# Loading the first block of Wk in two halves, and running its matmuls ahead of the second tile's transposes

## The chip, the core and the metric

The kernel runs on one core of a Trainium2 chip. The metric is the time of one execution on the device in microseconds (us); the median of seven executions stands for the kernel. A core has five engines that run side by side, each with its own instruction queue: TensorE (PE in the profile; PEld is its loading of weights), VectorE (DVE), ScalarE (ACT), GpSimd (POOL) and SyncE (SP). SP and ACT also issue the transfers between device memory and on-chip memory.

## The reference

One block of linear attention over 2048 rows of 640 values, with 32 heads of 20 values each. Everything is in bf16.

```python
qkv = (x @ wqkv).reshape(B, S, 3, H, Dh)      # B 1, S 2048, D 640, H 32, Dh 20
q, k, v = ...                                 # [B, H, S, Dh]
phi = lambda t: jnp.where(t > 0, t + 1, jnp.exp(t)) + 1e-6
pq, pk = phi(q), phi(k)
kv = jnp.einsum("bhsd,bhse->bhde", pk, v)
z = jnp.einsum("bhsd->bhd", pk)
num = jnp.einsum("bhqd,bhde->bhqe", pq, kv)
den = jnp.einsum("bhqd,bhd->bhq", pq, z)[..., None] + 1e-6
out = (num / den) -> [B, S, D] @ wo
```

## The kernel before

The 2048 rows of x are 16 tiles of 128 rows, and the 640 columns are 5 blocks of 128. K of a tile is 10 matmuls: for each block c of the contraction, two halves h of 320 output columns, accumulated in two banks of PSUM (`k_half`, L287 to L299; matmul on L292). The stationary operand is the transposed x of that tile and block (`xT`), the moving operand a half row of Wk's block c (`wk`). Then `k_phi` (L301) makes phi(K) on ScalarE and VectorE. After all K tiles come the state matmuls (L316), the Q tiles (L353), the folding of the state with V's weights and Wo, and the output matmuls (L575); these follow in an order written out as a string.

TensorE needs x transposed. For x tiles 2 to 15 transposing DMAs bring it straight into `xT` (`load_xT`, L186). For tiles 0 and 1 the rows are loaded plainly into `xn`, TensorE transposes them against an identity matrix (`transpose_x`, L192 to L212, matmul on L199), and the result is copied into `xT`: the first two blocks (part a) by VectorE (L211), the last three (part b) by ScalarE (L208).

The helper `P.add` gives every operation to one engine's queue in the order of the calls and works out the semaphore waits from the names that each operation reads and writes. So each queue is in order: an instruction that waits holds up those behind it on its engine. A transfer has a semaphore of its own.

The order of the first loads is written out in `load_wk` (L234). SP issues: left half of x tile 0, then Wk blocks 0, 2 and 3, each whole. ACT issues: right half of x tile 0, x tile 1, then Wk blocks 1 and 4. In the strings "w01 w23 w34" and "x12 w12 w45" the digits are the first block or tile and the one after the last. SP goes on with the transposing DMAs of x (L188), Wq, the rest of x, and the other weights.

TensorE begins with warm-up matmuls on constants (`warm`, L280), which have no use but to keep it busy; then it transposes tile 0, does one more warm-up matmul, and follows the string `order` (L629): `k00a` is K of tile 0 with block 0, first half; `t1a` is part a of the transposes of tile 1; without a last letter both halves are meant.

```python
        warm(5)
        warm(1, 128)
        for part in range(2):
            transpose_x(0, part)
        warm(1)
        order = "k00a t1a k00b t1b k10 k01 k11 k02 k12 k03 k13 k04 k14"
```

K of tiles 2 to 15 follows, tile by tile (L639 to L642).

Of the kernel before, what the change touches and what calls it, by code (L numbers as in the profile page):

```python
# [84 lines left out]
def bass_standalone__linear_attn_block__prompt_kernel(nc, x, wqkv, wo, out):  # L85
    B, S, D = x.shape
# [4 lines left out]
    HALF = D // 2  # L91
# [9 lines left out]
    with contextlib.ExitStack() as ctx:  # L101
        es = ctx.enter_context

        def sb(name, cols, dt=BF16):
            return es(nc.sbuf_tensor(name, [128, cols], dt))

        xT = sb("xT", NC_ * S)
        xn = sb("xn", NT * D)
        wk = sb("wk", NC_ * D)
# [29 lines left out]
        P = Plan(nc, es)  # L139

        def bank(b, n=BK, off=0, parts=128):
            return ps[0:parts, BK * b + off:BK * b + off + n]
# [49 lines left out]
        def transpose_x(st, part):  # L192
            lo, hi = ((0, 2), (2, NC_))[part]
            b = (6, 4)[st] + part
            v = bank(b, HALF).bitcast(BF16)

            def mm(e):
                for c in range(lo, hi):
                    r = e.transpose(  # L199
                        v[:, 128 * c:128 * c + 128],  # L200
                        xn[:, st * D + 128 * c:st * D + 128 * c + 128], ident[:, :])
                return r
            P.add("pe", mm, reads=xn_keys(st)[:1 + part] + ["ident"], writes=[("bank", b)])
            dst = xT[:, :].rearrange("p (c s) -> p c s", s=S)[
                :, lo:hi, 128 * st:128 * st + 128]
            src = v.rearrange("p (c s) -> p c s", s=128)[:, lo:hi, :]
            if part:
                P.add("act", lambda e: e.copy(dst, src),  # L208
                      reads=[("bank", b), "table"], writes=[("xT", st, lo)])
            else:  # L210
                P.add("dve", lambda e: e.tensor_copy(dst, src),  # L211
                      reads=[("bank", b)], writes=[("xT", st, lo)])  # L212

        def xT_keys(a, b, cs=range(NC_)):
            keys = []
            for i, (p, q) in enumerate(XCH):
                if p < b and a < q:
                    keys += [("xT", i)] if i >= NPE else sorted(
                        {("xT", i, 0 if c < 2 else 2) for c in cs})
            return keys  # L220
# [7 lines left out]
        def load_xn(a, b, eng):  # L228
            P.add(eng, lambda e: e.dma_start(
                xn[:, a * D:b * D].rearrange("p (t n) -> p t n", n=D),  # L230
                x[0, 128 * a:128 * b, :].rearrange("(t p) n -> p t n", p=128)),
                writes=[("xn", t) for t in range(a, b)], dma=True)

        def load_wk():  # L234
            tl = mybir.InstLoadActFuncSet(
                name=nc.get_next_instruction_name(),
                act_func_set_id=ACT_TABLE_SET_LN_EXP, ins=[], outs=[])
            P.add("act", lambda e: e.add_instruction(tl), writes=["table"])
            for eng, lo in (("sp", 0), ("act", HALF)):
                P.add(eng, lambda e, lo=lo: e.dma_start(  # L240
                    xn[:, lo:lo + HALF], x[0, 0:128, lo:lo + HALF]),
                    writes=[("xn", 0, lo)], dma=True)
            for eng, what in (("sp", "w01 w23 w34"), ("act", "x12 w12 w45")):
                for k in what.split():
                    a, b = int(k[1]), int(k[2])
                    if k[0] == "x":
                        load_xn(a, b, eng)
                    else:
                        P.add(eng, lambda e, a=a, b=b: e.dma_start(
                            wk[:, a * D:b * D].rearrange("p (c n) -> p c n", n=D),  # L250
                            wqkv[128 * a:128 * b, D:2 * D].rearrange("(c p) n -> p c n", p=128)),
                            writes=[("wk", c) for c in range(a, b)], dma=True)
# [27 lines left out]
        def warm(n, cols=BK):  # L280
            for _ in range(n):
                P.add("pe", lambda e: e.matmul(
                    bank(4, cols), nc.const_aps.tensor(1.0, [128, 128], BF16),
                    nc.const_aps.tensor(1.0, [128, cols], BF16), start=True, stop=True),
                    writes=[("bank", 4)])

        def k_half(st, h, cs=range(NC_)):  # L287
            b = 2 * (st % 4)

            def mm(e):  # L290
                for c in cs:
                    r = e.matmul(  # L292
                        bank(b + h, HALF),
                        xT[:, c * S + 128 * st:c * S + 128 * st + 128],
                        wk[:, c * D + HALF * h:c * D + HALF * (h + 1)],
                        start=(c == 0), stop=(c == NC_ - 1))
                return r
            P.add("pe", mm, reads=xT_keys(128 * st, 128 * st + 128, cs) + [("wk", c) for c in cs],
                  writes=[("bank", b + h)])  # L299

        def k_phi(st):  # L301
# [317 lines left out]

        pool_const()  # L620
        load_wk()
        load_xT()
        load_rest()
        warm(5)
        warm(1, 128)
        for part in range(2):
            transpose_x(0, part)
        warm(1)
        order = "k00a t1a k00b t1b k10 k01 k11 k02 k12 k03 k13 k04 k14"  # L629
        for k in order.split():  # L630
            st, part = int(k[1]), "ab".find(k[-1])
            if k[0] == "t":
                transpose_x(st, part)
            else:
                for h in range(2) if part < 0 else (part,):
                    k_half(st, h, (int(k[2]),))
        for st in range(2):
            k_phi(st)
        for st in range(2, NT):  # L639
            k_half(st, 0)  # L640
            k_half(st, 1)
            k_phi(st)  # L642
# [117 lines left out]
```

## Time and profile before

| what | value |
|---|---|
| median of 7 executions | 99.82 us (99.72 to 100.46) |
| the profiled execution | 100.11 us, with a span of 98.9 us |
| TensorE busy | 95.2 us, 96% of the span |
| VectorE, ScalarE, GpSimd busy | 62.0, 48.9, 4.5 us |
| K matmuls (L292) | 160, 22.2 us |
| bytes moved by DMA | 12.27 MB |
| first warm-up matmul | at 0.82 us |

The span runs from the first to the last instruction; the execution's own time is 1.2 us longer. Busy time of TensorE counts each matmul to its end, which is modelled, and neighbouring matmuls overlap. Times inside the span are counted from its start. "PE ps L292" in the profile is a matmul of line 292 that writes PSUM; "SPq" and "ACTq" are the issues of transfers on these two queues, and the number after the KB is the median time in us from the issue to the landing.

### The profile page before, as it was taken

The page shows a single profiled execution, that of the slowest core. Times are in us where ns is not written, and L with a number is a line of the kernel's source. Part 1 is how long each engine was busy: PE and PEld are TensorE (multiplying, and loading weights), DVE is VectorE, ACT ScalarE, POOL GpSimd, SP SyncE. Part 2 cuts the span into 40 slices and gives each one's busy share as a digit, 9 for nine tenths or more (in the row PEclk, how much of TensorE's full clock was granted, in tenths as well). Part 3 has the DMA queues.
Part 4 walks back from the last instruction along what each step waited for, and adds up shares of the span by engine and source line. Part 5 has one row for each costly group of instructions (what it writes and reads, how often), then busy time and mean ns, then how long its engine had stood idle before and what let it go on. Part 6 is the DMA issues. An engine that isn't in the chain of part 4 may idle for free.

```text
span 98.9 us, 1845 instructions
## 1 busy us (share of the span) xinstructions
PE 95.2 (96%) x709; PEld 61.1 (62%) x709; DVE 62.0 (63%) x124; ACT 48.9 (49%) x93; POOL 4.5 (5%) x19
## 2 busy tenths in 40 slices
PE   6799999999999999999999999999999999999991
PEld 2367777777755544445687857655557677777770
DVE  5314998888899439708837599758999207272112
ACT  5116455544526120005806557696988665453441
POOL 6400000000000000000000002400000000000000
PEclk9999999999999999999999999999999999999999
DMA  2999999999996169000000023313200326632334
GB/s 52 293 277 242 240 167 123 352 363 360 285 144 82 12 134 195 7 0 0 3 3 7 0 62 93 93 29 87 80 0 0 133 59 178 207 128 88 115 133 136
DMA packets 25104, 12.27 MB, mean 124 GB/s; under 512 B 17288, under 2 KB 25096, under 8 KB 25096
## 3 DMA queue, kind: packets, MB, share of 16 engines
q1 hardware_dynamic: 24376, 11.55, 48.6%
q10 hardware_dynamic: 720, 0.61, 1.9%
q8 instruction: 5, 0.08, 0.4%
q14 instruction: 3, 0.02, 0.1%
HBM read 5.90 MB, written 2.62 MB: 86 GB/s over the span
## 4 chain that ended last, share of the span: by engine, by line
PE 93%; DMA 4%; DVE 1%; SPq 0%; issue 0%
PE ps L292 22%; PE ps L575 22%; PE ps L316 22%; PE ps L353 22%; DMA wk<-in_wqkv_dram 4%; PE ps L444 1%; PE ps L543 1%; PE ps L471 1%; SPq L240 0%; DVE xT L211 0%; DVE osb L601 0%; PE ps L424 0%; PE ps L199 0%
## 5 line engine op out<-in xcount | busy, mean ns | idle before, releaser
L316 PE MATMUL ps<-pk,xn 128*128 128x480 bf16 (+1 forms) x160 | 23.2, 299 | 0.0
L353 PE MATMUL ps<-xT,wqn 128*128 128x512 bf16 x100 | 23.1, 379 | 0.0
L292 PE MATMUL ps<-wk,xT 128*128 128x320 bf16 x160 | 22.2, 299 | 0.7 <-DMA wk<-in_wqkv_dram 0.6
L575 PE MATMUL ps<-w2p,pq 128*128 128x320 bf16 (+2 forms) x170 | 22.1, 291 | 0.0
L292 PEld LDWEIGHTS ps<-wk,xT 128*128 128x128 bf16 x160 | 15.5, 98 | 7.4 <-DMA wk<-in_wqkv_dram 1.2
L575 PEld LDWEIGHTS ps<-w2p,pq 128*128 128x128 bf16 x170 | 15.9, 98 | 6.2 <-issue 0.2
L316 PEld LDWEIGHTS ps<-pk,xn 128*128 128x128 bf16 x160 | 13.5, 98 | 9.2 <-issue 0.3
L361 ACT ACTIVATE eq<-ps 128x512 bf16<-128x512 f32 x20 | 11.9, 597 | 14.0 <-PE ps L353 13.8
L353 PEld LDWEIGHTS ps<-xT,wqn 128*128 128x128 bf16 x100 | 11.4, 118 | 9.1 <-issue 0.3
L305 ACT ACTIVATE ek<-ps 128x640 bf16<-128x640 f32 x16 | 11.2, 704 | 10.8 <-PE ps L292 10.1
L598 ACT CAST osb<-ps 128x320 bf16<-128x320 f32 (+1 forms) x27 | 11.2, 417 | 9.4 <-PE ps L575 8.7
L310 DVE SCALAR_TENSOR_TENSOR pk<-ps,ek 128x640 bf16<-128x640 f32 x16 | 13.2, 825 | 0.5
L568 DVE TENSOR_TENSOR pq<-pq,rd 128x512 bf16<-128x512 bf16 x20 | 7.3, 419 | 5.1 <-DMA rd<-rdc 5.1
L307 DVE TENSOR_SCALAR ek<-ek 128x640 bf16<-128x640 bf16 x16 | 5.2, 324 | 5.1 <-ACT ek L305 4.9
L374 DVE TENSOR_SCALAR eq<-eq 128x512 bf16<-128x512 bf16 x20 | 5.8, 288 | 3.9 <-ACT eq L361 3.7
L601 DVE CAST osb<-ps 128x320 bf16<-128x320 f32 (+2 forms) x7 | 3.0, 431 | 8.3 <-PE ps L575 8.2
L365 ACT ACTIVATE rq<-ps 128x512 bf16<-128x512 f32 x13 | 7.7, 592 | 0.0
L338 ACT CAST pt<-ps 128x480 bf16<-128x480 f32 x4 | 2.3, 563 | 8.2 <-PE ps L316 8.1
L378 DVE TENSOR_TENSOR pq<-eq,rq 128x512 bf16<-128x512 bf16 x13 | 5.5, 425 | 1.1 <-ACT rq L365 0.7
L387 DVE TENSOR_TENSOR za<-pk 128x1280 f32<-128x1280 bf16 x4 | 5.8, 1483 | 0.0
L381 DVE SCALAR_TENSOR_TENSOR pq<-ps,eq 128x512 bf16<-128x512 f32 x7 | 4.8, 691 | 0.2
L387 DVE TENSOR_TENSOR za<-za 128x1280 f32<-128x1280 f32 x3 | 4.5, 1486 | 0.0
(41 smaller groups left out, 36.0 us busy)
## 6 DMA issues: line engine op xcount, KB each, us to landing
out_dram<-osb SPq DMA_DIRECT2D x15, 160.0 KB, 1.8
xn<-in_x_dram SPq DMA_DIRECT2D x2, 640.0 KB, 8.6
xn<-in_x_dram SPq DMA_DIRECT2D x1, 960.0 KB, 7.8
wqn<-in_wqkv_dram SPq DMA_DIRECT2D x1, 800.0 KB, 5.7
wog<-in_wo_dram SPq DMA_DIRECT2D x2, 375.0 KB, 5.4
w2p<-w2g SPq DMA_DIRECT2D x10, 75.0 KB
wv<-in_wqkv_dram SPq DMA_DIRECT2D x5, 120.0 KB, 5.4
rd<-rdc SPq DMA_DIRECT2D x8, 64.0 KB, 2.2
```

What stands on the lines that cost most here:

```text
L292: r = e.matmul(bank(b + h, HALF), xT[:, c * S + 128 * st:c * S + 128 * st + 128], wk[:, c * D + HALF * h:c * D + HALF * (h + 1)], start=(c ...
L305: P.add("act", lambda e: e.activation(fold(t[:, :]), two_banks(b), ACTF.Exp), reads=banks + ["table"], writes=[("ek", st % 3)])
L310: P.add("dve", lambda e: e.scalar_tensor_tensor(fold(pk[:, st * D:(st + 1) * D]), two_banks(b), 0.0, fold(t[:, :]), ALU.max, ALU.add), rea ...
L316: return e.matmul(bank(d // PB[h], PW[h], off=PW[h] * (d % PB[h])), xn[:, st * D + 128 * d:st * D + 128 * d + 128], pk[:, st * D + PO[h]:s ...
L353: r = e.matmul(bank(b), wqn[:, d * D:(d + 1) * D].rearrange("p (q c) -> p c q", c=NC_)[:, c, :], xT[:, d * S + BK * sbk:d * S + BK * (sbk ...
L361: P.add("act", lambda e: e.activation(t[:, :], bank(b), ACTF.Exp), reads=[("bank", b), "table"], writes=[("eq", i)])
L365: P.add("act", lambda e: e.activation(r[:, :], bank(b), ACTF.Relu), reads=[("bank", b), "table"], writes=[("rq", i)])
L374: P.add("dve", lambda e: e.tensor_scalar(t[:, :], t[:, :], 1.0, 1e-6, ALU.min, ALU.add), reads=[("eq", i)], writes=[("eq", i)])
L387: P.add("dve", lambda e: e.tensor_tensor(d_ap, a, b, ALU.add), reads=ra + rb, writes=[dst])
L568: P.add("dve", lambda e: e.tensor_tensor(v, v, rd[i][:, BK * h:BK * (h + 1)], ALU.mult), reads=[("rd", i, 2 * h), ("rd", i, 2 * h + 1), (" ...
L575: r = e.matmul(bank(b, hi - lo), pq[:, c * S + 128 * st:c * S + 128 * st + 128], w2p[:, c * D + lo:c * D + hi], start=(c == 0), stop=(c == ...
L598: P.add("act", lambda e: e.copy(osb[j][:, lo:hi], bank(b, hi - lo)), reads=[("bank", b)], writes=keys)
```

## The change

Wk's block 0 is no longer one transfer on SP. It is loaded as two halves of 320 columns, the left one by SP and the right one by ACT, each directly behind that queue's half of x tile 0. Block 1 moves from ACT to SP, block 2 from SP to ACT. SP then issues x tile 0 left, Wk 0 left, Wk 1, Wk 3; ACT issues x tile 0 right, Wk 0 right, x tile 1, Wk 2, Wk 4. A K matmul with block 0 waits for its own half only. On TensorE the last warm-up matmul has 256 columns instead of 512; both matmuls of tile 0 with block 0 stand ahead of the transposes of tile 1, which are no longer interleaved with them; and tile 0's matmuls with block 1 stand ahead of tile 1's with block 0.

```diff
-            for eng, lo in (("sp", 0), ("act", HALF)):
-                P.add(eng, lambda e, lo=lo: e.dma_start(
-                    xn[:, lo:lo + HALF], x[0, 0:128, lo:lo + HALF]),
-                    writes=[("xn", 0, lo)], dma=True)
-            for eng, what in (("sp", "w01 w23 w34"), ("act", "x12 w12 w45")):
+            for key, t, src in ((("xn", 0), xn, x[0, 0:128, :]), (("wk", 0), wk, wqkv[0:128, D:2 * D])):
+                for eng, lo in (("sp", 0), ("act", HALF)):
+                    P.add(eng, lambda e, t=t, src=src, lo=lo: e.dma_start(
+                        t[:, lo:lo + HALF], src[:, lo:lo + HALF]),
+                        writes=[key + (lo,)], dma=True)
+            for eng, what in (("sp", "w12 w34"), ("act", "x12 w23 w45")):
...
-            P.add("pe", mm, reads=xT_keys(128 * st, 128 * st + 128, cs) + [("wk", c) for c in cs],
+            P.add("pe", mm, reads=xT_keys(128 * st, 128 * st + 128, cs) + [("wk", c) if c else ("wk", 0, HALF * h) for c in cs],
...
-        warm(1)
-        order = "k00a t1a k00b t1b k10 k01 k11 k02 k12 k03 k13 k04 k14"
+        warm(1, 256)
+        order = "k00 t1a t1b k01 k10 k11 k02 k12 k03 k13 k04 k14"
```

## The prediction

> **What bounds the kernel now.** I read the chain of waits first, because it tells which engine has to be shortened at all.
>
> ```profile
> PE 93%; DMA 4%; DVE 1%; SPq 0%; issue 0%
> ...
> 0.79 0.39 SPq L240
> ...
> 1.24 3.50 DMA wk<-in_wqkv_dram
> ...
> 4.79 0.31 PE ps L292
> 5.10 0.16 PE ps L199 x2
> ...
> 5.28 0.30 DVE xT L211
> ...
> 5.63 21.64 PE ps L292 x158
> ```
>
> The columns are start and length in us. From 5.63 us to the last eviction the chain never leaves TensorE. So whatever happens before 5.63 us moves the end one for one, as long as TensorE finds its operands after that point. Before it the chain is one transfer, Wk block 0 (issued 1.24, landed 4.74), then the transposes of x tile 1 and VectorE's copy of them. Next I read the timeline of TensorE in that stretch (start, length, line, operation, count, idle before and what ended it):
>
> ```profile
> 3.02 0.73 PE L199 MATMUL ps<-ident,xn 128*128 128x128 bf16 x5
> 3.55 0.63 PE L282 MATMUL ps<-const-bfloat16-1.0 128*128 128x512 bf16 x1
> 4.79 0.31 PE L292 MATMUL ps<-wk,xT 128*128 128x320 bf16 x1 [0.61 <-DMA wk<-in_wqkv_dram]
> 4.96 0.28 PE L199 MATMUL ps<-ident,xn 128*128 128x128 bf16 x2
> 5.08 0.30 PE L292 MATMUL ps<-wk,xT 128*128 128x320 bf16 x1
> 5.21 0.33 PE L199 MATMUL ps<-ident,xn 128*128 128x128 bf16 x3
> 5.63 8.60 PE L292 MATMUL ps<-wk,xT 128*128 128x320 bf16 x62
> ```
>
> The two K matmuls of block 0 (4.79 and 5.08) already stand among tile 1's transposes. The last line gives the pace: (8.60 - 0.30) / 61 = 0.136 us for one K matmul. Third, the DMA queue's issues with their landings, and the busy time by stage (last two columns: mean DMA share and GB/s):
>
> ```profile
> wk<-in_wqkv_dram SPq DMA_DIRECT2D x3, 160.0 KB, 3.9
> wk<-in_wqkv_dram ACTq DMA_DIRECT2D x2, 160.0 KB, 4.3
> xn<-in_x_dram ACTq DMA_DIRECT2D x1, 160.0 KB, 3.7
> ...
> 1.80:2.70 0.90, 0.90 (x4) 0.29 (x2) 0.90 (x1) 0.26 (x1) 0.82 (x3) 1.00 0.98 215
> 2.70:3.10 0.40, 0.40 (x3) 0.08 (x2) 0.24 (x1) 0.00 (x0) 0.27 (x2) 1.00 0.58 163
> 3.10:3.60 0.50, 0.50 (x8) 0.45 (x6) 0.13 (x1) 0.00 (x0) 0.43 (x2) 1.00 1.05 353
> 3.60:4.20 0.60, 0.58 (x3) 0.00 (x0) 0.17 (x1) 0.41 (x1) 0.29 (x2) 1.00 0.95 254
> 4.20:5.40 1.20, 0.61 (x7) 0.47 (x7) 0.12 (x1) 0.07 (x1) 0.00 (x0) 1.00 1.01 355
> ```
>
> Issue start plus issue-to-landing, one transfer at a time, gives pairs, one member on each queue: the halves of x tile 0 at 3.0 and 3.2; Wk 0 (SP) and x tile 1 (ACT) at 4.74 and 4.9; Wk 2 and Wk 1 at 5.6 and 5.8; Wk 3 and Wk 4 at 6.5 and 6.7. The second and later pairs are 320 KB each. The last two each took 0.9 us, which is 364 GB/s and fits the 355 of the table. The first such pair took 1.7 us; its extra 0.8 us is the stretches with 163 and 254 GB/s. Transfers are the limit of this prologue.
>
> [...] five transposes starting at 3.02 have the span 0.73 us (0.11 apart), three at 5.21 have 0.33 us (0.055 apart), and the first warm-up matmul began at 0.82.
>
> **The change, part by part.**
>
> *Wk block 0 as two halves behind x tile 0.* ACT gets one more issue (0.39 us by the row of L240) ahead of x tile 1, so x tile 1 is issued at about 1.65 instead of 1.23. SP's third issue becomes Wk 1, at about 1.66 against 1.71 from ACT. SP still has four loads before the DMA transposes, so these are issued at 2.65 as now. ACT's own next work, the copy at 3.79, is behind issues that now end at about 3.1 instead of 2.65: hidden. Landing of block 0: before 4.74 in any case, since fewer bytes are ahead of it; at the earliest about 3.5 (x tile 0 at 3.1 plus 160 KB at 364 GB/s). Its two matmuls cost 2 x 0.27 at half clock, or 0.27 in all at full clock. At the latest they end near 5.1 to 5.3, at the earliest 4.4.
>
> *x tile 1 and Wk 1 become the next pair.* In front of them are now 160 KB (x tile 0) and 160 KB (block 0). From 3.1, the mean landing of x tile 0: 0.82 for the slow stretch, if it stays (the next pair's mean, 4.82, is 1.72 later, of which 0.9 is the fair price), and 480 KB at 364 GB/s, 1.35 us, gives 5.27 as the mean of the pair. SP's member lands about 0.09 before the mean and ACT's 0.09 after: Wk 1 at 5.2, x tile 1 at 5.36. That is 0.5 us later for x tile 1 than now (4.9).
>
> *The order on TensorE.* Now: transposes from 4.96, K matmuls of tile 1 from 5.63 (0.67 later: two transposes, drain, VectorE's copy of 0.29, semaphore), then 18 K matmuls to the end of tile 1: 5.63 + 18 x 0.136 = 8.08. Afterwards: first transpose at 5.36 + 0.05 = 5.41; five of them, 5 x 0.056, end at 5.69; the two matmuls of block 1 for tile 0 follow at once (Wk 1 is there) and end at 5.96; tile 1's first needs the copy, 5.41 + 0.67 = 6.08, so 0.12 is idle; 16 are left: 6.08 + 16 x 0.136 = 8.26. The new order thus hides 0.27 of the copy's wait, but starts 0.45 later: net +0.18 us. Break-even is x tile 1 landing at 5.2.
>
> *What is late next.* Wk 2, now on ACT behind x tile 1, with Wk 3 as partner: 5.27 + 0.9 + 0.09 = 6.3; wanted at 6.08 + 4 x 0.136 = 6.6. Wk 3 is wanted at 7.2, and lands about 6.1. Wk 4, now alone beside the DMA transposes: not later than another 0.9 us, 7.2, wanted at 7.7. x tile 2's transpose (2.65 + 4.7 = 7.35 now) is wanted at 8.26. All covered by 0.3 us or more; if that cover goes, the cost is what it overshoots.
>
> *The shorter warm-up (256 columns).* It takes 256 columns away in a stretch where TensorE is idle anyway, 0.21 us at half clock. Gain nothing. [...]
>
> Sum: +0.18 us. The profiled execution took 100.11 us (98.9 span, 1.2 around it), 0.29 above the median of 99.82; the difference is carried to the median: 100.0 us. What a measurement of this kernel can tell from no change is about 0.3%, 0.3 us, so the likeliest case is inside that.
>
> **Rivals.**
>
> *Later: x tile 1 takes the place of Wk 1 in more than bytes.* If landing is paced from the issue, x tile 1, now third on ACT's queue, has the 4.1 us of the third transfer there (Wk 1 now: 1.71 to 5.8). 1.65 + 4.1 = 5.75; first transpose at 5.80, which is 0.39 after my case: +0.57, 100.39 us. It decides against me from a landing of about 5.5 (+0.3). For it: the landings from issue grow steadily along each queue (2.4, 3.7, 4.1, 4.5), and there are nine transfers instead of eight. Against: 160 KB fewer lie ahead than lay ahead of Wk 1.
>
> *Faster: the slow stretch shrinks.* If the 0.82 us lies in the shadow of block 0, for which TensorE does not hurry any more, all but 0.2 may go: pair at 4.65, x tile 1 at 4.74, first transpose at 4.79, end of tile 1 at 7.64: -0.44, 99.38 us. For it: 163 GB/s in 2.70 to 3.10 is partly ACT's queue waiting for x tile 1. Against: the same queue still has one transfer behind another there, with half the bytes to fill it.
>
> [...] Less warm-up, and TensorE idle from about 4.4 to 5.4 instead of 4.2 to 4.8. [...] Against: until 4.4 it is as busy as now, since the two matmuls of block 0 fill what the warm-up lost.
>
> *That the change does nothing of what it says* can be excluded: the instruction order has both block 0 matmuls ahead of the five transposes.
>
> **How the numbers follow.** My case 0.52, its own range 99.75 to 100.3; the later landing 0.30; the faster one 0.13; the clock 0.05. Faster by over 0.3% is nearly all of the fast rival: 0.12. Slower: most of the later landing (0.27), the clock (0.05) and the upper end of my case (0.08): 0.40. The rest, 0.48, is within 0.3%. The range goes from the fast rival to above the later landing, 99.4 to 100.65, and leaves out the clock case and tails of both.
>
> **What will show it.** Right: x tile 1 lands at 5.2 to 5.6, the first transpose of it at about 5.41 and TensorE's idle time before it is put down to xn, not wk; block 0's matmuls end before 5.3; after the first K matmul of tile 1 (about 6.1) no gap. Wrong: x tile 1 before 5.2 (faster), Wk 1 or Wk 2 ending a wait on TensorE, or K matmuls 0.27 apart after 6 us (clock).

## The result and the profile after

The change made the kernel slower: ratio to the kernel before 1.0088, 95% interval 1.0067 to 1.011. The profiled execution took 100.70 us with a span of 99.5 us (before 100.11 and 98.9). Over all executions the medians are 102.31 us (25 executions, 100.55 to 104.16) and 100.06 us (62), and the ratio is smaller than these two give because it leaves out, on both sides, the executions that lie well above the fastest ones (13 of the 25 here, of 102.31 us or more; only three of the 62 before took over 102).

The chain of waits of the changed kernel (start and length in us):

```profile
1.24 0.46 ACTq L241
...
1.72 4.20 DMA xn<-in_x_dram
...
5.97 0.45 PE ps L199 x5
6.42 21.58 PE ps L293 x158
28.00 2.03 PE ps L317 x10
```

The transfer at its head is no longer Wk block 0 but x tile 1: issued at 1.72, behind ACT's half of block 0, and landed at 5.92. Before, it landed at 4.9. From there the chain is TensorE alone, as before; the state matmuls (L317) start at 28.00, where before they started at 27.27 (5.63 + 21.64, the last line of the chain that the prediction shows). So the loss is complete by then: 0.73 us. It is still 0.74 at the last output matmuls (77.59 before, 78.33 now); the span is only 0.6 longer because the end after them came 0.15 sooner in this execution. TensorE's timeline in the same stretch:

```profile
3.55 0.42 PE L283 MATMUL ps<-const-bfloat16-1.0 128*128 128x256 bf16 x1
3.92 0.71 PE L293 MATMUL ps<-wk,xT 128*128 128x320 bf16 x2
5.97 0.45 PE L199 MATMUL ps<-ident,xn 128*128 128x128 bf16 x5 [1.33 <-DMA xn<-in_x_dram]
6.26 8.03 PE L293 MATMUL ps<-wk,xT 128*128 128x320 bf16 x57
```

Block 0's matmuls do run early, from 3.92. Then TensorE stands idle for 1.33 us, and the releaser is x tile 1. Tile 0's matmuls with block 1, which stand behind tile 1's transposes in the queue, could not go ahead of them: Wk 1 had landed at 5.7 (1.70 + 4.0), and they began at 6.26. In this execution TensorE works at two rates: five transposes take 0.74 us at 3.01 and 0.45 at 5.97. The prediction calls them half and full clock; the granted clock reads 1.00 at both times, so below they are the lower and the higher rate. The issues, with KB each and us to landing, and the stages (sum of the stage, busy of PE, PEld, DVE, ACT, POOL, clock, DMA share, GB/s):

```profile
xn<-in_x_dram ACTq DMA_DIRECT2D x1, 160.0 KB, 4.2
...
wk<-in_wqkv_dram SPq DMA_DIRECT2D x1, 80.0 KB, 2.6
wk<-in_wqkv_dram ACTq DMA_DIRECT2D x1, 80.0 KB, 2.8
```

```profile
2.70:3.10 0.40, 0.40 (x3) 0.15 (x2) 0.24 (x1) 0.00 (x0) 0.27 (x2) 1.00 1.39 298
3.10:3.60 0.50, 0.50 (x8) 0.49 (x5) 0.13 (x1) 0.00 (x0) 0.43 (x2) 1.00 0.56 62
```

The halves of block 0 come quickly, 298 GB/s in 2.70 to 3.10 where 163 flowed before. Then little moves: 62 GB/s in 3.10 to 3.60, where 353 flowed before. Over these 0.9 us the kernel before moved 242 KB (0.4 x 163 + 0.5 x 353), the changed one 150 KB. The DMA engines are not simply idle in this time: their busy share over the 0.9 us is 0.93 ((0.4 x 1.39 + 0.5 x 0.56) / 0.9), and before it was 0.84 (a packet counts with its whole time where it starts, so a share can be over 1). So packets were under way, but slow. The stretch from 3.1 us to the landing of x tile 1, before and after:

```profile
3.10:4.93 1.83, 1.22 (x9) 0.55 (x7) 0.29 (x1) 0.48 (x1) 0.73 (x3) 1.00 1.01 321
```

```profile
3.10:5.92 2.82, 1.54 (x10) 0.70 (x7) 0.29 (x1) 0.48 (x1) 0.73 (x3) 1.00 0.91 282
```

About 590 KB moved in the first (1.83 x 321) and about 800 KB in the second (2.82 x 282), so x tile 1 shares the engines with loads that were issued behind it.

### The profile page after: what moved, and what is told of

The parts are those of the page before. It is cut to its first block, busy times and chain, and to the rows that moved or that the text cites. A ratio compares the mean times of both kernels' runs of the same rounds, so it can differ in the third digit from the quotient of the medians.

```text
span 99.5 us, 1846 instructions
## 1 busy us (share of the span) xinstructions
PE 95.3 (96%) x709; PEld 61.2 (62%) x709; DVE 62.0 (62%) x124; ACT 48.9 (49%) x93; POOL 4.5 (4%) x19
## 4 chain that ended last, share of the span: by engine, by line
PE 92%; DMA 4%; ACTq 0%; ACT 0%; DVE 0%; issue 0%
PE ps L576 22%; PE ps L317 22%; PE ps L354 22%; PE ps L293 22%; DMA xn<-in_x_dram 4%; PE ps L445 1%; PE ps L544 1%; PE ps L472 1%; ACTq L241 0%; PE ps L199 0%; ACT L238 0%; DVE osb L602 0%; PE ps L425 0%
## 5 line engine op out<-in xcount | busy, mean ns | idle before, releaser
L317 PE MATMUL ps<-pk,xn 128*128 128x480 bf16 (+1 forms) x160 | 23.2, 299 | 0.0
L317 PEld LDWEIGHTS ps<-pk,xn 128*128 128x128 bf16 x160 | 13.5, 98 | 9.2 <-issue 0.3
```

What stands on the lines that cost most here:

```text
L317: return e.matmul(bank(d // PB[h], PW[h], off=PW[h] * (d % PB[h])), xn[:, st * D + 128 * d:st * D + 128 * d + 128], pk[:, st * D + PO[h]:s ...
```

## The experiments

The theories. The slot theory: x tile 1 is late because it is now the third transfer issued on its queue; what is issued third, at about 1.7 us, lands late however few bytes lie ahead. The rivals: the bytes ahead of it count, at 364 GB/s; or the new order on TensorE does the harm; or TensorE, idle for longer, works at the lower rate afterwards (the prediction's clock case).

**Loads of after, order and warm-up of before (e1_loads).**

```diff
-        warm(1, 256)
-        order = "k00 t1a t1b k01 k10 k11 k02 k12 k03 k13 k04 k14"
+        warm(1)
+        order = "k00a t1a k00b t1b k10 k01 k11 k02 k12 k03 k13 k04 k14"
```

> The changed loads with the order and the warm-up of the kernel before. Slot theory (x tile 1 lands late because it is issued third on ACT's queue): x tile 1 lands at about 5.9 us as in the changed kernel, the first K matmul of tile 1 runs 0.67 us after the first transpose, 18 K matmuls follow it instead of 16: the end of tile 1 at 5.97 + 0.67 + 18 x 0.136 = 9.1 us against 8.8, so 0.3 us slower than the changed kernel, a ratio to before of about 1.010 to 1.012. Rival (the new order on TensorE does the harm): near the kernel before, 1.000 to 1.003.

Ratio 1.0085 (1.0044 to 1.0126). Its chain:

```profile
1.73 4.14 DMA xn<-in_x_dram
...
6.58 2.48 PE ps L293 x17
```

x tile 1 lands at 5.87 again, so the loads alone bring the whole loss. That it would be 0.3 us slower than the changed kernel can't be told with this interval, which rests on two executions.

**Loads of before, new order and warm-up (e2_order).** The mirror image: the diff above with plus and minus exchanged, in the kernel before.

> The loads of the kernel before with the new order and the shorter warm-up. Slot theory: block 0 at 4.74 us, transposes of tile 1 from 5.06, block 1 lands at 5.8 as before and holds its two matmuls to 5.86, tile 1's first K matmul at 6.13 and the end of tile 1 at 8.3: 0.2 us slower than before, ratio 1.001 to 1.004. Rival (order does the harm): as slow as the changed kernel, about 1.009.

Ratio 1.0009 (0.9983 to 1.0036). The order is not what costs. Here x tile 1, second on ACT, took 3.3 us to land, and the last wait is Wk 1 (1.73 + 3.90 = 5.63).

**Only the split undone (e3_whole).** Block 0 whole on SP; Wk 1 stays on SP and Wk 2 on ACT.

```diff
-            for eng, what in (("sp", "w01 w23 w34"), ("act", "x12 w12 w45")):
+            for eng, what in (("sp", "w01 w12 w34"), ("act", "x12 w23 w45")):
```

(against the kernel before; order and warm-up as changed)

> Only the split is undone: block 0 whole on SP behind x tile 0, so x tile 1 is second on ACT's queue again; block 1 on SP, block 2 on ACT, order and warm-up as changed. Slot theory: x tile 1 lands at about 4.9 us, block 1 at 5.6, end of tile 1 at 8.1 to 8.2: ratio 1.000 to 1.003. Rival (moving block 1 to SP and block 2 to ACT, or the order, costs the time): 1.005 to 1.009.

Ratio 0.9999 (0.997 to 1.0028): the whole loss is gone. From its issues and its timeline:

```profile
xn<-in_x_dram ACTq DMA_DIRECT2D x1, 160.0 KB, 2.9
```

```profile
4.48 0.74 PE L199 MATMUL ps<-ident,xn 128*128 128x128 bf16 x5
5.51 6.66 PE L292 MATMUL ps<-wk,xT 128*128 128x320 bf16 x47 [0.29 <-DMA wk<-in_wqkv_dram]
```

x tile 1 lands 2.9 us after its issue at 1.24, its transposes are at 4.48, and Wk 1 is the last wait. The split is thus the part that costs, and through x tile 1.

**Fewer bytes in the same slots (e4_narrow).** Block 0 of Wk is left out of the result.

```diff
-                        t[:, lo:lo + HALF], src[:, lo:lo + HALF]),
+                        t[:, lo:lo + (64 if t is wk else HALF)], src[:, lo:lo + (64 if t is wk else HALF)]),
...
-                        wk[:, c * D + HALF * h:c * D + HALF * (h + 1)],
+                        (wk if c else xn)[:, c * D + HALF * h:c * D + HALF * (h + 1)],
```

> As the changed kernel, but each half of block 0 loads 64 of its 320 columns, and the matmuls with block 0 take x tile 0 instead of it (block 0 of Wk is left out of the result). The transfers, their issue slots and all waits stay; 128 KB fewer bytes lie ahead of x tile 1. Slot theory (pace from the issue): x tile 1 still lands at 5.7 to 5.9 us, ratio 1.007 to 1.009. Bytes theory (364 GB/s): it lands 0.35 us earlier, about 5.55, ratio about 1.005.

Ratio 1.0036 (1.0001 to 1.007), from three executions. It is below what the slot theory gave and nearer to the bytes theory. The chain and the stages:

```profile
1.72 3.99 DMA xn<-in_x_dram
```

```profile
2.70:3.10 0.40, 0.40 (x3) 0.03 (x2) 0.24 (x1) 0.00 (x0) 0.28 (x2) 1.00 0.93 109
3.10:3.60 0.50, 0.50 (x8) 0.43 (x6) 0.10 (x1) 0.00 (x0) 0.43 (x2) 1.00 0.85 87
```

With 128 KB less ahead of it x tile 1 lands at 5.71, 0.21 earlier, not 0.35, and far from the 4.1 to 4.9 of a second slot. But the five profiled executions with the changed loads unaltered (the changed kernel, e1_loads, e5_fill, e8_k10, e11_fill_k10) landed it between 5.74 and 6.35, and this profiled execution is the longest of the three that the ratio rests on, by 0.24 us. So this run doesn't tell how much the 128 KB count. The two stretches carry 109 and 87 GB/s, at a DMA share of 0.93 and 0.85: here too the engines have packets under way and little comes through.

**One small transfer more in the kernel before (e6_extra, and e12_extra_fill with filler on TensorE).**

```diff
+        dum = sb("dum", 64)
...
+            P.add("act", lambda e: e.dma_start(dum[:, :], wqkv[0:128, D + HALF:D + HALF + 64]),
+                  writes=["dum"], dma=True)
             for eng, what in (("sp", "w01 w23 w34"), ("act", "x12 w12 w45")):
```

> The kernel before with one more transfer of 16 KB on ACT's queue between the right half of x tile 0 and x tile 1; its data is used by nothing. Slot theory: x tile 1 is third on ACT and lands at 5.4 to 5.7 us instead of 4.2 to 4.9, block 1 fourth and lands near 6.3; 16 matmuls of 0.136 are left behind block 1: end of tile 1 at 6.35 + 18 x 0.136 = 8.6 to 8.8, 0.5 to 0.7 us slower, ratio 1.005 to 1.007. Bytes theory: 16 KB at 364 GB/s are 0.05 us: ratio 1.000 to 1.001.

> The kernel before with the 16 KB transfer ahead of x tile 1 on ACT, and five filler matmuls on TensorE ahead of tile 1's transposes. Slot theory: x tile 1 lands at about 5.7 us and block 1 at 6.4, end of tile 1 at 6.45 + 18 x 0.136 = 8.9: 0.8 us slower than before, ratio 1.006 to 1.010. Bytes theory: 1.000 to 1.001.

e6_extra 1.0145 (1.0092 to 1.0198), e12_extra_fill 1.0157 (1.0125 to 1.0188). The chain of e12_extra_fill, and the timeline line of e6_extra where x tile 1's transposes begin:

```profile
1.71 4.70 DMA xn<-in_x_dram
```

```profile
5.78 0.39 PE L200 MATMUL ps<-ident,xn 128*128 128x128 bf16 x2 [1.34 <-DMA xn<-in_x_dram]
```

16 KB, worth 0.05 us at 364 GB/s, moved x tile 1 from 4.9 to 5.7 and 6.4, and made the kernel before slower than the changed one (e12_extra_fill). The bytes theory, which gave 1.001 at most, can't survive this run. The size was above the expected ratio in both; x tile 1 in e12_extra_fill landed 0.7 later than expected. In e6_extra a part of it is TensorE's lower rate: its two transposes take 0.39 us, where they take 0.28 in the kernel before. One rival was not tested: each of these loads is 144 packets whatever its width (the queue with ACT's bytes has 576 packets up to 7 us for four loads, and 720 for five in the changed kernel and in e4_narrow alike). A cost for each packet ahead, in place of one for each transfer ahead, would give the same in e4_narrow, e6_extra and e12_extra_fill.

**Filler for the idle TensorE (e5_fill).**

```diff
-        order = "k00 t1a t1b k01 k10 k11 k02 k12 k03 k13 k04 k14"
+        order = "k00 f t1a t1b k01 k10 k11 k02 k12 k03 k13 k04 k14"
...
+            if k == "f":
+                warm(5)
+                continue
```

> The changed kernel with five more warm-up matmuls between block 0's matmuls and the transposes of tile 1, where TensorE is idle from 4.5 to 6.0 us. Slot theory: nothing changes in the landing of x tile 1 (about 5.9 us); same as the changed kernel, ratio to before 1.007 to 1.010. Rival [...]: the filler wins back a part, ratio 1.004 or less.

Ratio 1.009 (1.0065 to 1.0114). x tile 1 lands at 6.03, and keeping TensorE busy wins nothing against this comparison: a lower rate after the wait is not in the 1.0088. Its six executions lie between 100.79 and 101.27 us (on this see the clock case below).

**Tile 1's block 0 ahead of tile 0's block 1 (e8_k10, and e11_fill_k10 with the filler).**

```diff
-        order = "k00 t1a t1b k01 k10 k11 k02 k12 k03 k13 k04 k14"
+        order = "k00 t1a t1b k10 k01 k11 k02 k12 k03 k13 k04 k14"
```

> The changed kernel with tile 1's block 0 matmuls ahead of tile 0's block 1 matmuls, as in the kernel before. If the new order hides what the prediction said, the two matmuls of 0.136 no longer cover the copy's wait: the end of tile 1 comes 0.27 us later than in the changed kernel, ratio to before about 1.011. If it hides nothing: about 1.009.

> The changed kernel with the five filler matmuls, and tile 1's block 0 matmuls ahead of tile 0's block 1 matmuls. If the new order hides 0.27 us of the copy's wait: 0.27 us slower than the variant with the filler alone (1.009), ratio about 1.0115. If it hides nothing: 1.009.

e8_k10 came out at 1.0242 (1.0208 to 1.0277), more than either guess. Its timeline says why that can't be used for the order:

```profile
5.79 0.72 PE L199 MATMUL ps<-ident,xn 128*128 128x128 bf16 x5 [1.18 <-DMA xn<-in_x_dram]
6.57 7.60 PE L293 MATMUL ps<-wk,xT 128*128 128x320 bf16 x47
```

Five transposes take 0.72 us, as tile 0's do at 3.04 us in this run, where the changed kernel's took 0.45. In this execution TensorE was at the lower rate when x tile 1 came. With the filler, e11_fill_k10, the ratio is 1.0133 (1.0106 to 1.016), against 1.009 for the filler alone. Its timeline:

```profile
6.41 0.45 PE L199 MATMUL ps<-ident,xn 128*128 128x128 bf16 x5
7.08 7.10 PE L293 MATMUL ps<-wk,xT 128*128 128x320 bf16 x51 [0.22 <-DVE xT L211]
```

TensorE now waits for the copy (0.22 idle) and 18 matmuls are left behind it, not 16: the direction is as expected. The size isn't separated: of the 0.43 us between the two ratios, x tile 1's landing at 6.35 instead of 6.03 accounts for 0.32 in the profiled executions.

**Block 1 in halves (e7_split1).** On e3_whole, Wk 1 as two column halves in the third slots.

```diff
-            for eng, what in (("sp", "w01 w12 w34"), ("act", "x12 w23 w45")):
+            for eng, what in (("sp", "w01 h0 w23"), ("act", "x12 h1 w34 w45")):
...
+                    if k[0] == "h":
+                        lo = HALF * int(k[1])
+                        P.add(eng, lambda e, lo=lo: e.dma_start(
+                            wk[:, D + lo:D + lo + HALF], wqkv[128:256, D + lo:D + lo + HALF]),
+                            writes=[("wk", 1, lo)], dma=True)
...
```

> As the variant with block 0 whole and block 1 on SP, but block 1 is loaded as two column halves, third on both queues; block 2 fourth on SP, blocks 3 and 4 fourth and fifth on ACT. Slot theory: the halves land at about 5.1 us instead of 5.5, block 2 at about 6.0; TensorE's stream starts 0.3 us earlier and waits for block 2 hardly at all: end of tile 1 at 7.7 instead of 8.0, ratio 0.996 to 0.999. Rival (half the bytes in a slot land no sooner, or the later blocks stall): 1.000 to 1.004.

Ratio 1.0 (0.9971 to 1.003). The halves did land early:

```profile
wk<-in_wqkv_dram SPq DMA_DIRECT2D x1, 80.0 KB, 3.2
wk<-in_wqkv_dram ACTq DMA_DIRECT2D x1, 80.0 KB, 3.4
```

From issues at 1.7 that is 4.9 and 5.1, against 5.5 for the whole block in e3_whole, and in its timeline the stream of K matmuls starts at 5.34:

```profile
4.81 0.74 PE L199 MATMUL ps<-ident,xn 128*128 128x128 bf16 x5
5.34 8.93 PE L298 MATMUL ps<-wk,xT 128*128 128x320 bf16 x61
```

That is 0.17 us before e3_whole, but the state matmuls begin at 27.45, against 27.25 there: the transposes are still at the lower rate (0.74 us for five), and no gain can be measured. A third slot is thus not late whatever it carries: with half the bytes in the transfers themselves they landed 0.4 to 0.6 us sooner, in one trace each.

**x tile 1 on a third queue (e9_pool, e10_pool2).**

```diff
                 reads=["ident"], writes=["ident"])
+            load_xn(1, 2, "pool")
...
-            for eng, what in (("sp", "w12 w34"), ("act", "x12 w23 w45")):
+            for eng, what in (("sp", "w12 w34"), ("act", "w23 w45")):
```

(e10_pool2 also loads Wk 1 as halves in the third slots.)

> The changed kernel with x tile 1 issued by GpSimd directly after the identity matrix is made (at about 1.5 us), so that it stands behind nothing on ACT; block 2 and block 4 move up one place on ACT. Slot theory with a pace for each queue: x tile 1 lands by about 4.5 us, block 1 (third on SP) at 5.4 to 5.7 becomes the last wait: end of tile 1 at 8.0 to 8.2, ratio 0.999 to 1.002. Rival (all queues share one pace, so only the place among all transfers counts): x tile 1 lands at 5.3 or later, ratio 1.005 or more.

> As the run with x tile 1 on GpSimd, and block 1 in two column halves as well, third on both queues; block 2 fourth on SP, blocks 3 and 4 fourth and fifth on ACT. Slot theory: block 0 at 3.9, x tile 1 by 4.5, the halves of block 1 at 5.1: TensorE's stream starts at about 5.1 instead of 5.6 and may wait a little for block 2 (about 5.9): ratio 0.996 to 0.999. Rival: three queues at once slow each other, or block 2 lands past 6.3: 1.000 to 1.004.

Both were slower than before: 1.0206 (1.0145 to 1.0268) and 1.0105 (1.0059 to 1.0152). From the issues of e9_pool:

```profile
xn<-in_x_dram POOLq DMA_DIRECT2D x1, 160.0 KB, 4.8
```

Issued at 1.72 on an otherwise empty queue, x tile 1 lands at 6.5, as late as third on ACT, as the rival in the expectation said. My theory of a pace for each queue falls: place on ACT's queue is not the cause by itself. Either what is issued around 1.7 us lands late on any queue, or GpSimd's path is slow for another reason; these runs don't tell the two apart. In both profiled executions TensorE was at the lower rate for a part of the time after x tile 1's landing (the K matmuls recorded up to 14.3 us come 0.165 us apart on average in e9_pool, 7.24 us for 43, and 0.18 in e10_pool2, 7.26 for 39, where the kernel before has 0.136), so their landings count here and not their times.

## Why the prediction was wrong

**The step that failed** is the landing of x tile 1: "0.82 for the slow stretch, if it stays", and 480 KB at 364 GB/s, which gave "Wk 1 at 5.2, x tile 1 at 5.36". It landed at 5.92. I took the prologue to be limited by the bytes ahead, and moved the slow stretch along unchanged. Shown in its place: x tile 1 is issued 0.49 us later (1.72 against 1.23), and it also takes longer from its issue, 4.0 to 4.7 us third on ACT in eight kernels, against 2.9 to 3.7 second on ACT in four. In the same eight 62 to 189 GB/s moved between 3.10 and 3.60 us, in the four 297 to 376. 16 KB ahead do what 80 KB do (e6_extra, e12_extra_fill).

Two readings behind that step don't come out. At 364 GB/s the stretches with 163 and 254 GB/s lose 0.22 and 0.18 us, 0.40 together and not 0.82. And pairs do not land one after the other with only the bytes ahead of them moved: from 3.1 us to the landing of x tile 1 about 590 KB moved in the kernel before, where the pairs up to then have 320, and about 800 in the changed one, where the prediction counted 480. The 92 KB that the changed kernel lacks by 3.6 us are worth 0.25 us at 364 GB/s, under half of the 0.56 that the landing was missed by. Why little moves between 3.1 and 3.6 us, and whether the place on the queue, the time of issue or the number of packets decides, stays open.

**Block 0 hidden:** right. Its halves landed at 3.8 and 4.0, between the bounds given, and its two matmuls were over long before x tile 1.

**The order on TensorE:** right in its form. From the first transpose (5.97) to tile 1's first K matmul the prediction had 0.67 us, and 2.85 to the end of tile 1 (8.26 - 5.41). From 5.97 that gives 8.82, 0.74 after 8.08, and 0.73 was measured where the state matmuls start. Only the start was wrong.

**Late next:** right. Neither Wk 1, Wk 2 nor the transposing DMA ends a wait on TensorE after 6 us.

**The rival "later":** the nearest. It gave a landing at 5.75 and 100.39 us, from the third transfer's 4.1 us on ACT; measured 4.2. Its argument, time from the issue, is what the landings follow; my reason against it (160 KB fewer lie ahead) is the one that e6_extra and e12_extra_fill refute. Even so it falls short: the landing came 0.17 us after its 5.75, which with its +0.57 makes the 0.74 of the chain, and the ratio says 0.88%. The changed loads gave landings from 5.74 to 6.35 us in other profiled executions, which would cover the rest. That last is argued, not shown for each execution.

**Faster:** excluded; the stretch in which little moves came 0.4 us later, while TensorE had other work, but it did not shrink as that rival said. That the 163 GB/s were partly ACT's queue waiting for x tile 1 was my estimate and is not shown.

**The clock case:** not in the 1.0088 (e5_fill), but its price is shown by two pairs of kernels that differ in the filler alone. The K matmuls from the chains of e8_k10 (without) and e11_fill_k10 (with filler):

```profile
6.57 22.68 PE ps L293 x158
```

```profile
7.08 21.63 PE ps L293 x158
```

In e6_extra and e12_extra_fill it is 22.80 and 21.64. So about 1.1 us go when TensorE is at the lower rate after its wait for x tile 1. What sets the rate is not shown: TensorE was idle for 1.18 us before x tile 1 in e8_k10 and for 1.34 in e6_extra, and 1.33 in the changed kernel and 1.47 in e1_loads, which kept the higher rate. The chance of 0.05 was my estimate and may have been too small: of the 13 executions that the ratio leaves out, five have a granted clock of 0.983, and with filler (e5_fill, e11_fill_k10) none of twelve took more than 101.55 us. That the lower rate is behind these 13 is not shown, since none of them has a trace, and the profiled executions of e8_k10 and e6_extra have a granted clock of 1.0.

No version here beats the kernel before; e3_whole and e7_split1 equal it.

## What to carry to other kernels

In this prologue of a few transfers, time from issue was a better measure than bytes in front: 16 KB more ahead moved a landing by 0.8 and 1.5 us. So look up, in the trace, how long the first, second and third transfer of each queue take to land, and give the early slots to what ends the chain. Judge by more than one trace: the same loads landed x tile 1 up to 0.6 us apart. Here splitting a block in two so that its first use comes sooner took a slot from what stood behind it (x tile 1, issued at 1.72 instead of 1.23); as that one was on the chain, the block's earlier arrival was worth nothing. An interleaving that was possible because two operands landed together can mean that both are critical; then nothing is won by pulling one ahead.

## What the runs showed that was not expected

- A transfer of 16 KB ahead of another moved that one's landing by 0.8 to 1.5 us (4.9 to 5.7 in e6_extra, 6.4 in e12_extra_fill).
- After the smaller early transfers little moves for a while, although packets are under way: 62 GB/s for half a microsecond in the changed kernel, 87 and 109 in e4_narrow (DMA share 0.85 and 0.93), against 353 in the kernel before.
- A plain load issued by GpSimd (e9_pool) kept that engine for 0.71 us (0.45 for the same load on ACT in the changed kernel) and landed 4.8 us after its issue.
